# Transposing two slabs by whole 128x128 products instead of 32-row strips, with fewer filler products and another written order

## The chip, the core and the metric

The kernel runs on one core of a Trainium2 chip. The core has TensorE (matrix products into PSUM, written PE in the profile, its weight loads PEld), VectorE (DVE), ScalarE (ACT), GpSimd (POOL) and SyncE (SP), which here only issues DMAs. Each engine works through its own list of instructions in order and waits on semaphores for the others. The metric is the device time of one execution in microseconds (us).

## What is computed

Two layers, each an attention block and a gated block, over 2048 rows of 512 values in bfloat16; both layers use the same weights.

```python
x = x + A(layernorm(x));  x = x + B(layernorm(x))      # twice

# A: 32 heads of 16
q, k, v = split(x @ wqkv)
pq, pk  = q @ w_phi, k @ w_phi                         # per head
phi     = concat(softmax(p), softmax(-p))              # 32 features for q and for k
kv, z   = sum_s phi_k^T v, sum_s phi_k
o       = (phi_q @ kv) / (phi_q . z + 1e-6)
A       = o @ wo

# B
gate = x @ W_gate;  up = x @ W_up
B    = (relu(gate) * up) @ W_down
```

Attention is linear: the sums `kv` and `z` need all rows of keys and values before any row of the output can be made.

## The kernel before

The 2048 rows are 16 tiles of 128 rows, grouped into five slabs of 2, 4, 4, 4 and 2 tiles (`SLABS`). Slabs are numbered 0 to 4, layers 0 and 1. A stage is named by its layer and slab: `a01` is the normalization ahead of the attention of layer 0, slab 1; `g12` that ahead of the gated block of layer 1, slab 2.

At the start the kernel folds `w_phi` into the key and query weights (`fold`): it transposes the weights (keys by TensorE, queries by DMA), multiplies them by a block diagonal of `w_phi`, and evicts the results into `Wkp` and `Wqp`. Ahead of that TensorE runs eight warming products (`warm`, L788) and two groups of fillers (`filler`, L793, products of 256 columns whose result nobody reads): 8 before the fold and 10 after the fold of the keys.

`layernorm` (L862 to L908) takes a slab's tiles: statistics on VectorE (L847, L872), the reciprocal deviation on ScalarE (L874, L876), and the normalization of each tile into `ytile` on the engine that the table `ENG` names under `ap/...` (L889 or L892; on ScalarE it needs one small VectorE instruction more, L881). The normalized tile must then lie transposed in `yA` or `yG`. There are three ways: a DMA transpose from SyncE's queue (stages in `XPOSE`); for steps of several tiles `strips` (L910 to L930), which turns the tiles with 32x32 transposes at four row positions, 16 for each tile, into four banks, each bank then evicted by one copy that `ENG` places under `yc/...`; for steps of one tile, four 128x128 transposes into one bank (L713) and one copy. Before the change the strips are used by `a01` and `a02`: 64 transposes each (L921). All four copies of the strips together complete every tile; a tile's copy in the third way completes that tile alone.

`keys` makes, tile by tile, keys and values (L709 with `Wkp` and `wv`, eight products of 512 columns), exponentials on ScalarE (L949), their sums by a reduction on VectorE (L955), reciprocals (L958, or L961 and L962 on ScalarE by `rz/...`), the value eviction (`vc/...`), and the scaled values (L969, on GpSimd or VectorE by `vh/...`); then TensorE sums keys times values in 32 small products a tile (L981). For tile 9 of layer 0 the reduction is replaced by two DMA transposes and eight products on TensorE (`sums_by_pe`, L999 and L1007, by `zk/9`). `queries` (L1050) and `attend` follow, the gated block is `glu`.

The order of the instructions is settled while the kernel is built. `Program.schedule` (L446) plays the operations through with a cost for each; among those that can start it takes the one that starts first and, of equals, the one with the lowest number in `TURNS`, one number for each operation. The lists of the five engines come out in the order of the planned starts, and `plan` adds the semaphore waits. The planner has a cost for TensorE's instructions, which come in pieces: it takes a new piece to be there `FETCH0` ns after the piece before was entered, or `FETCH` ns once its clock is past 25 us. `LATE` is added to the planned landing of DMA transposes and some other DMAs. These numbers emit nothing; they only move the order.

Of the kernel before, what the change touches and what calls it, by code (L numbers as in the profile page):

```python
# [23 lines left out]
ENG = {'ap/a00/0': 'act',  # L24
 'ap/a01/1': 'dve',
# [4 lines left out]
 'ap/a03/3': 'dve',  # L30
 'ap/a10/0': 'act',
 'ap/a10/1': 'pool',
 'ap/a11/0': 'pool',
 'ap/a11/3': 'act',
 'ap/a12/1': 'pool',
 'ap/a12/3': 'act',
 'ap/a13/3': 'act',
 'ap/a14/1': 'act',
 'ap/g01/0': 'act',
 'ap/g01/1': 'act',  # L40
 'ap/g02/0': 'act',
 'ap/g02/1': 'act',
 'ap/g02/3': 'act',
 'ap/g03/0': 'act',
 'ap/g03/2': 'act',
# [3 lines left out]
 'ap/g12/3': 'act',  # L49
 'ap/g13/0': 'act',  # L50
 'ap/g14/1': 'act',
# [7 lines left out]
 'es/02/1': 'pool',  # L59
 'es/03/0': 'pool',  # L60
 'es/03/3': 'pool',
 'es/04/1': 'pool',
 'es/04/3': 'pool',
 'es/12/0': 'pool',
 'es/12/2': 'pool',
 'es/12/3': 'pool',
 'es/13/0': 'pool',
 'es/13/1': 'pool',
 'es/13/3': 'pool',
 'fck1': 'act',  # L70
 'fck2': 'dve',
 'fck3': 'act',
 'fcq2': 'dve',
 'ftk2': 'dve',
 'ftk3': 'act',
 'ld/wphi': 'sp',
 'ms/BD': 'pool',
 'ms/ZO 0': 'pool',
 'ms/kvs eps 0': 'pool',
 'ms/kvs eps 1': 'pool',  # L80
# [3 lines left out]
 'ot/00/3': 'act',  # L84
 'ot/01/0': 'dve',
 'ot/02/2': 'dve',
 'ot/03/0': 'dve',
 'ot/04/1': 'dve',
 'ot/04/2': 'dve',
 'ot/04/3': 'dve',  # L90
 'ot/11/0': 'dve',
 'ot/11/2': 'dve',
 'ot/12/2': 'dve',
 'ot/12/3': 'dve',
 'ot/13/0': 'dve',
 'ot/13/2': 'dve',
 'ot/13/3': 'dve',
 'ot/14/2': 'dve',
 'rz/0/1': 'act',
 'rz/0/12': 'act',  # L100
 'rz/0/13': 'act',
# [4 lines left out]
 'rz/0/6': 'act',  # L106
 'rz/0/7': 'act',
 'rz/1/14': 'act',
 'rz/1/15': 'act',
 'rz/1/2': 'act',  # L110
 'rz/1/4': 'act',
 'rz/1/6': 'act',
 'rz/1/7': 'act',
 'rz/1/8': 'act',
 'vc/0/11': 'dve',
 'vc/0/2': 'dve',
 'vc/0/5': 'dve',
 'vc/0/8': 'dve',
 'vc/1/12': 'dve',
 'vc/1/7': 'dve',  # L120
 'vc/1/8': 'dve',
 'vh/0/10/0': 'dve',
 'vh/0/11/0': 'dve',
 'vh/0/12/0': 'dve',
 'vh/0/13/0': 'dve',
# [5 lines left out]
 'vh/0/4/0': 'dve',  # L131
 'vh/0/5/0': 'dve',
 'vh/0/5/1': 'dve',
 'vh/0/7/1': 'dve',
 'vh/1/0/0': 'dve',
 'vh/1/11/0': 'dve',
 'vh/1/12/0': 'dve',
 'vh/1/12/1': 'dve',
 'vh/1/13/0': 'dve',
 'vh/1/14/0': 'dve',  # L140
 'vh/1/15/0': 'dve',
 'vh/1/15/1': 'dve',
 'vh/1/2/0': 'dve',
 'vh/1/2/1': 'dve',
 'vh/1/3/0': 'dve',
 'vh/1/4/0': 'dve',
 'vh/1/5/0': 'dve',
 'vh/1/5/1': 'dve',
 'vh/1/6/1': 'dve',
 'vh/1/8/0': 'dve',  # L150
# [5 lines left out]
 'yc/a01/03': 'act',  # L156
# [11 lines left out]
 'yc/a14/1': 'dve',  # L168
 'yc/g00/1': 'dve',
# [5 lines left out]
 'yc/g10/0': 'dve',  # L175
# [6 lines left out]
 'za/03': 'dve',  # L182
 'za/11': 'dve',
 'za/12': 'dve',
 'zk/9': 'pe'}
# [422 lines left out]
def build_kernel(nc, A_x, A_wqkv, A_w_phi, A_wo, W_gate, W_up, W_down, out):  # L608
# [8 lines left out]
    with ExitStack() as ctx:  # L617
# [86 lines left out]
        def bank(name):  # L704
            return Bank(name, pb)
# [13 lines left out]
        def b16half(ps):  # L719
            return ps.b16()[:, 0:512]  # L720
# [671 lines left out]
```

## Time and profile before

| | us |
|---|---|
| three runs | 388.72, 388.75, 387.99 |
| median | 388.72 |
| profiled execution | 388.32 |
| its span | 386.5 |
| TensorE busy | 371.2 |
| VectorE busy | 277.8 |
| ScalarE busy | 196.1 |
| GpSimd busy | 66.5 |

The span runs from the first to the last instruction of the profile; the profiled execution has its own time, 1.8 us above the span. In the lines of the profile that follow, a line of the timeline gives the start, the duration, the engine, the line of the kernel, what is written from what, a count, and in brackets the idle time of the engine before it with what ended that time. A line of the waits gives who waited for whom, the total, the number of times and the longest. A line of the windows gives the stretch, its length, and for TensorE's products, TensorE's weight loads, VectorE, ScalarE and GpSimd the busy time and in brackets the number of instructions; then the clock granted to TensorE, the busy share of the DMA engines, and GB/s.

### The profile page before, as it was taken

The page shows a single profiled execution, that of the slowest core. Times are in us where ns is not written, and L with a number is a line of the kernel's source. Part 1 is how long each engine was busy: PE and PEld are TensorE (multiplying, and loading weights), DVE is VectorE, ACT ScalarE, POOL GpSimd, SP SyncE. Part 2 cuts the span into 40 slices and gives each one's busy share as a digit, 9 for nine tenths or more (in the row PEclk, how much of TensorE's full clock was granted, in tenths as well). Part 3 has the DMA queues.
Part 4 walks back from the last instruction along what each step waited for, and adds up shares of the span by engine and source line. Part 5 has one row for each costly group of instructions (what it writes and reads, how often), then busy time and mean ns, then how long its engine had stood idle before and what let it go on. Part 6 is the DMA issues. An engine that isn't in the chain of part 4 may idle for free.

```text
span 386.5 us, 9068 instructions
## 1 busy us (share of the span) xinstructions
PE 371.2 (96%) x3743; PEld 197.6 (51%) x3793; DVE 277.8 (72%) x566; ACT 196.1 (51%) x433; POOL 66.5 (17%) x59
## 2 busy tenths in 40 slices
PE   7898999999999999999999999999999999999996
PEld 4453555484445444454457555466444444454574
DVE  7998998995856775974769797688865465743333
ACT  5998879752553434532535398982444113323111
POOL 2081730020502500120024031005024000000000
PEclk9999999999999999999999999999999999999999
DMA  7993402053661020202100310314562140230011
GB/s 227 303 323 67 70 5 55 25 156 61 139 97 52 22 54 3 54 15 54 27 4 2 62 29 6 83 42 136 102 151 70 44 83 1 44 91 16 2 41 50
DMA packets 58058, 27.72 MB, mean 72 GB/s; under 512 B 40384, under 2 KB 56352, under 8 KB 58016
## 3 DMA queue, kind: packets, MB, share of 16 engines
q1 hardware_dynamic: 57584, 26.77, 28.9%
q8 instruction: 30, 0.49, 0.6%
q10 hardware_dynamic: 432, 0.36, 0.3%
q14 instruction: 12, 0.10, 0.1%
HBM read 14.73 MB, written 4.00 MB: 48 GB/s over the span
## 4 chain that ended last, share of the span: by engine, by line
PE 86%; ACT 5%; DVE 3%; DMA 2%; issue 2%; SPq 1%; DVEq 0%; ACTq 0%
PE pb L709 82%; ACT expq L1050 2%; PE pb L981 2%; DMA hT<-in_A_wqkv_dram 1%; PE pb L1139 1%; DMA yG<-ytile 1%; DVE x_sb L1209 1%; ACT vsb L823 1%; ACT abT L823 1%; DVE stats L847 0%; PE pb L1078 0%; ACT expk L949 0%; ACT ytile L889 0%; SPq L732 0%; DVE hT L1263 0%
## 5 line engine op out<-in xcount | busy, mean ns | idle before, releaser
L709 PE MATMUL pb<-Wd,hT 128*128 128x512 bf16 (+3 forms) x353 | 93.1, 372 | 0.9 <-issue 0.6
L709 PE MATMUL pb<-yG,Wu 128*128 128x512 bf16 (+1 forms) x393 | 92.8, 336 | 0.8 <-DVE yG L820 0.3
L709 PE MATMUL pb<-yG,Wg 128*128 128x512 bf16 (+1 forms) x393 | 91.8, 336 | 0.4 <-issue 0.2
L1261 ACT ACTIVATE gate_sb<-pb 128x512 bf16<-128x512 f32 x80 | 46.6, 596 | 84.4 <-PE pb L709 51.8
L1263 DVE TENSOR_TENSOR hT<-gate_sb,pb 128x512 bf16<-128x512 bf16 x80 | 53.3, 682 | 39.4 <-PE pb L709 29.3
L1209 DVE TENSOR_TENSOR x_sb<-x_sb,pb 128x512 bf16<-128x512 bf16 x59 | 39.3, 680 | 23.2 <-PE pb L709 23.0
L709 PEld LDWEIGHTS pb<-yG,Wu 128*128 128x128 bf16 x400 | 39.0, 98 | 31.9 <-issue 0.5
L709 PEld LDWEIGHTS pb<-yG,Wg 128*128 128x128 bf16 x400 | 38.6, 98 | 29.9 <-issue 0.8
L709 PEld LDWEIGHTS pb<-Wd,hT 128*128 128x128 bf16 (+1 forms) x363 | 34.8, 98 | 36.6 <-issue 0.9
L969 POOL TENSOR_TENSOR vhat<-vsb,rZk 128x544 bf16<-128x544 bf16 x26 | 28.1, 1101 | 107.8 <-ACT vsb L823 58.6
L847 DVE BATCH_NORM_STATS2 stats<-x_sb 128x6 f32<-128x512 bf16 x60 | 39.8, 679 | 0.5 <-DMA x_sb<-in_A_x_dram 0.2
L709 PE MATMUL pb<-wv,yA 128*128 128x512 bf16 x124 | 37.3, 379 | 0.3 <-issue 0.2
L709 PE MATMUL pb<-Wkp,yA 128*128 128x512 bf16 x122 | 36.3, 379 | 1.1 <-ACT vsb L823 0.6
L1050 ACT ACTIVATE expq<-pb 128x512 bf16<-128x512 f32 x64 | 34.9, 631 | 3.6 <-PE pb L709 3.4
L709 PE MATMUL pb<-yA,Wqp 128*128 128x512 bf16 (+1 forms) x150 | 32.8, 334 | 2.9 <-issue 2.4
L709 PE MATMUL pb<-wo_sb,oT 128*128 128x512 bf16 x122 | 35.1, 379 | 0.6 <-ACT oT L823 0.5
L1172 POOL TENSOR_TENSOR expq<-expq,abT 128x1024 bf16<-128x1024 bf16 (+1 forms) x11 | 21.3, 1947 | 82.4 <-DVE nmr L881 30.5
L949 ACT ACTIVATE expk<-pb 128x512 bf16<-128x512 f32 x40 | 22.1, 612 | 10.8 <-PE pb L709 10.6
L955 DVE TENSOR_REDUCE Zk<-expk 128x64 f32<-128x1024 bf16 x19 | 22.7, 1201 | 5.8 <-ACT expk L949 5.7
L889 ACT ACTIVATE ytile<-x_sb,nmr,rstd 128x512 bf16<-128x512 bf16 x27 | 21.4, 815 | 5.8 <-DVE nmr L881 5.8
L709 PEld LDWEIGHTS pb<-yA,Wqp 128*128 128x128 bf16 x160 | 14.2, 98 | 14.2 <-issue 3.1
L709 PE MATMUL pb<-Wl,yG 128*128 128x192 bf16 x128 | 20.1, 246 | 0.4 <-DVE stats L847 0.2
(109 smaller groups left out, 372.7 us busy)
## 6 DMA issues: line engine op xcount, KB each, us to landing
abT<-spread SPq DMA_DIRECT2D x32, 128.0 KB
out_dram<-x_sb SPq DMA_DIRECT2D x15, 128.0 KB, 1.7
x_sb<-in_A_x_dram SPq DMA_DIRECT2D x3, 512.0 KB
Wu<-in_B_W_up_dram SPq DMA_DIRECT2D x1, 1280.0 KB
Wg<-in_B_W_gate_dram SPq DMA_DIRECT2D x1, 1280.0 KB
Wd<-in_B_W_down_dram SPq DMA_DIRECT2D x1, 1280.0 KB, 13.7
sums_scr<-abT SPq DMA_DIRECT2D x5, 256.0 KB, 2.3
Zs<-sums_scr SPq DMA_DIRECT2D x5, 256.0 KB, 2.7
```

What stands on the lines that cost most here:

```text
L709: op("pe", lambda e: e.matmul(view(ps), lhsT, rhs, start=start, stop=stop), reads=reads, writes=[ps], occ=max(25.0, 0.4167 * n + 2.6), lat ...
L823: op("act", lambda e: e.activation(dst(), src(), ACT.Copy), reads=[ps] + reads, writes=writes, occ=115 + 0.714 * n, lat=240 + 0.714 * n, n ...
L847: op("dve", lambda e: e.bn_stats(stats[:, t, :], src()), reads=[res], writes=[R("st", t)], occ=580, lat=680, name=f"bn{t}")
L889: op("act", (lambda t, yb: lambda e: e.activation(ytile[:, yb, :], x_sb[:, t, :], ACT.Identity, bias=nmr[:, t, :], scale=rstd[:, t, :]))(t ...
L949: op("act", (lambda i, s, pk: lambda e: e.activation(expk(i)[:, s, :], full(pk), ACT.Exp, scale=1.0 - 2.0 * s))(i, s, pk), reads=[pk], wri ...
L955: op("dve", (lambda i, zb: lambda e: e.tensor_reduce(Zk[:, zb, :], expk(i).rearrange("p s (h f) -> p (s h) f", f=16), AX.X, ALU.add))(i, z ...
L969: op(eng, (lambda i, s, vb, rz: lambda e: e.tensor_tensor(vhat(i)[:, s], vsb[:, vb, :, :], rZk[:, rz, s * 32:(s + 1) * 32].unsqueeze(2).to ...
L1050: op("act", (lambda c0, s, ps: lambda e: e.activation(eqv(st)[:, c0:c0 + per, s, :], ps.f32()[:, 0:per * n].rearrange("p (c n) -> p c n", ...
L1172: op(eng, lambda e: e.tensor_tensor(part, part, abT[:, c].rearrange("p (s n) -> p s n", s=2)[:, :, 0:n], ALU.mult), reads=Re + [R("abT", c ...
L1209: op("dve", lambda e: e.tensor_tensor(x_sb[:, t, :], x_sb[:, t, :], full(ps), ALU.add), reads=[R("x", t), ps], writes=[R("x", t)], occ=597 ...
L1261: op("act", (lambda gb, pg, k: lambda e: e.activation(gate_sb[:, gb, 0:k], pg.f32()[:, 0:k], ACT.Relu))(gb, pg, k), reads=[pg], writes=[R( ...
L1263: op("dve", (lambda gb, hb, pu, k: lambda e: e.tensor_tensor(hT[:, hb, 0:k], gate_sb[:, gb, 0:k], pu.f32()[:, 0:k], ALU.mult))(gb, hb, pu, k),
```

## The change

Two stages, `a01` and `a02`, are named in a new tuple `PLAIN`. `layernorm` no longer sends these through `strips`; it transposes each of their four tiles by four 128x128 products into a bank of its own and evicts that bank by one copy. The fillers after the fold of the keys go from 10 to 4, so that there are 12 and not 18. In the planner a piece of TensorE's instructions now counts as there 9000 ns after the piece before was entered if that was before 20 us of its clock, 6600 ns if before 29.5 us, and 3700 ns after. `LATE` goes from 300 to 400. `ENG` and `TURNS` are replaced: about a hundred operations move to another engine, and the order is written anew for all. `TURNS` itself is left out below.

```diff
 ENG = {
- 'ap/a00/0': 'act',
+ 'ap/a04/0': 'pool',
...
- 'ap/g01/0': 'act', 'ap/g01/1': 'act', 'ap/g02/0': 'act', 'ap/g02/1': 'act',
- 'ap/g02/3': 'act', 'ap/g03/0': 'act', 'ap/g03/2': 'act',
+ 'ap/g01/3': 'act', 'ap/g04/0': 'act', 'ap/g04/1': 'act',
...
- 'es/02/1': 'pool', 'es/03/0': 'pool', 'es/03/3': 'pool',
- 'es/12/0': 'pool', 'es/12/2': 'pool', 'es/13/0': 'pool',
+ 'es/13/2': 'pool', 'es/14/0': 'pool', 'es/14/1': 'pool', 'es/14/2': 'pool', 'es/14/3': 'pool',
- 'fck3': 'act', 'fcq2': 'dve', 'ftk2': 'dve',
+ 'ftk1': 'act', 'ld/x0': 'act',
- 'ms/ZO 0': 'pool', 'ms/kvs eps 0': 'pool', 'ms/kvs eps 1': 'pool',
+ 'ms/kvs 0 1': 'pool',
...
- 'vc/0/11': 'dve', 'vc/0/8': 'dve',
+ 'vc/0/3': 'dve', 'vc/0/4': 'dve', 'vc/0/9': 'dve',
...
- 'yc/a01/03': 'act',
+ 'yc/a01/03': 'dve',
+ 'yc/a02/00': 'dve', 'yc/a02/01': 'dve', 'yc/a02/02': 'dve', 'yc/a02/03': 'dve',
...
- 'zk/9': 'pe'}
...
+PLAIN = ()
...
-ZALL=(...); LASTCUT=((0,384),(384,512)); FILL=(8,10); LATE=300; LOADLATE=(150,200)
+ZALL=(...); LASTCUT=((0,384),(384,512)); LOADLATE=(150,200); FILL=(14,8); PLAIN=('a01','a02'); LATE=400; FILL=(8,4)
...
-    FETCH, FETCH0 = 3700.0, 9000.0
+    FETCH, FETCH1, FETCH0 = 3700.0, 6600.0, 9000.0
...
-                    came = crossed + (self.FETCH if at > 25000.0 else self.FETCH0) if chunk > self.CHUNK0 else 0.0
+                    came = crossed + (self.FETCH0 if crossed < 20000.0 else self.FETCH1 if crossed < 29500.0 else self.FETCH) if chunk > self.CHUNK0 else 0.0
...
-                elif step > 1:
+                elif step > 1 and key not in PLAIN:
                     strips(key, gi, b, r0, ybs)
                 else:
-                    ps = bank(f"ytr{t0}")
-                    for c in range(NC):
-                        tr(ps, ..., ytile[:, ybs[0], c * 128:(c + 1) * 128], [R("y", ybs[0])], f"ytr{t0}")
-                    evict(ENG.get(f"yc/{key}/{gi}", "act"), ..., 512, ps, [], R_yT(b, r0), f"ycp{t0}", False)
+                    for j, yb in enumerate(ybs):
+                        ps = bank(f"ytr{t0 + j}")
+                        for c in range(NC):
+                            tr(ps, ..., ytile[:, yb, c * 128:(c + 1) * 128], [R("y", yb)], f"ytr{t0 + j}")
+                        evict(ENG.get(f"yc/{key}/{gi}" + (f"{j}" if step > 1 else ""), "act"), ..., 512, ps, [], R_yT(b, r0 + j), f"ycp{t0 + j}", False)
                 t0 += step
```

Where `ENG` has no entry, a default holds: in the strips of `a01` and `a02` VectorE for the copies, in the plain way ScalarE; VectorE for the normalization of `a00` and ScalarE for that of the other layer 0 attention stages; SyncE for the load of the first tile; VectorE for the small fills, for the reduction of tile 9 and for the odd evictions of the fold of the keys, ScalarE for the fold's other evictions; VectorE for the scaling of the queries (`es/...`) and for the normalization ahead of the gated block.

More of the change, by code (lines that the diff above doesn't have):

```diff
@@ L23 @@
 HOLD = {}
-ENG = {'ap/a00/0': 'act',
- 'ap/a01/1': 'dve',
+ENG = {'ap/a01/1': 'dve',
  'ap/a01/2': 'dve',
@@ L33 @@
  'ap/a11/0': 'pool',
- 'ap/a11/3': 'act',
- 'ap/a12/1': 'pool',
+ 'ap/a11/1': 'pool',
+ 'ap/a12/0': 'act',
+ 'ap/a12/2': 'act',
  'ap/a12/3': 'act',
[L37 to L45, printed above, removed]
+ 'ap/a13/0': 'act',
+ 'ap/a13/2': 'pool',
+ 'ap/g01/3': 'act',
+ 'ap/g04/0': 'act',
+ 'ap/g04/1': 'act',
  'ap/g11/0': 'act',
@@ L48 @@
  'ap/g11/3': 'act',
- 'ap/g12/3': 'act',
- 'ap/g13/0': 'act',
- 'ap/g14/1': 'act',
+ 'ap/g12/0': 'act',
+ 'ap/g12/1': 'act',
+ 'ap/g13/2': 'act',
+ 'ap/g14/0': 'act',
  'em/01/01': 'dve',
@@ L58 @@
  'em/11/03': 'dve',
- 'es/02/1': 'pool',
- 'es/03/0': 'pool',
- 'es/03/3': 'pool',
+ 'em/11/13': 'dve',
  'es/04/1': 'pool',
  'es/04/3': 'pool',
- 'es/12/0': 'pool',
- 'es/12/2': 'pool',
  'es/12/3': 'pool',
- 'es/13/0': 'pool',
  'es/13/1': 'pool',
+ 'es/13/2': 'pool',
  'es/13/3': 'pool',
+ 'es/14/0': 'pool',
+ 'es/14/1': 'pool',
+ 'es/14/2': 'pool',
+ 'es/14/3': 'pool',
  'fck1': 'act',
  'fck2': 'dve',
- 'fck3': 'act',
- 'fcq2': 'dve',
- 'ftk2': 'dve',
+ 'ftk1': 'act',
  'ftk3': 'act',
  'ld/wphi': 'sp',
+ 'ld/x0': 'act',
  'ms/BD': 'pool',
- 'ms/ZO 0': 'pool',
- 'ms/kvs eps 0': 'pool',
- 'ms/kvs eps 1': 'pool',
+ 'ms/kvs 0 1': 'pool',
  'ot/00/0': 'dve',
@@ L83 @@
  'ot/00/2': 'dve',
[L84 to L87, printed above, removed]
+ 'ot/01/1': 'dve',
+ 'ot/01/2': 'dve',
+ 'ot/01/3': 'dve',
+ 'ot/02/1': 'dve',
+ 'ot/03/2': 'dve',
+ 'ot/03/3': 'dve',
  'ot/04/1': 'dve',
- 'ot/04/2': 'dve',
  'ot/04/3': 'dve',
- 'ot/11/0': 'dve',
+ 'ot/10/0': 'dve',
+ 'ot/10/3': 'act',
  'ot/11/2': 'dve',
- 'ot/12/2': 'dve',
- 'ot/12/3': 'dve',
- 'ot/13/0': 'dve',
+ 'ot/12/0': 'dve',
+ 'ot/13/1': 'dve',
  'ot/13/2': 'dve',
  'ot/13/3': 'dve',
- 'ot/14/2': 'dve',
+ 'ot/14/0': 'dve',
+ 'ot/14/3': 'dve',
  'rz/0/1': 'act',
+ 'rz/0/11': 'act',
  'rz/0/12': 'act',
- 'rz/0/13': 'act',
  'rz/0/14': 'act',
@@ L105 @@
  'rz/0/5': 'act',
- 'rz/0/6': 'act',
  'rz/0/7': 'act',
+ 'rz/0/9': 'act',
+ 'rz/1/0': 'act',
+ 'rz/1/10': 'act',
+ 'rz/1/11': 'act',
+ 'rz/1/12': 'act',
+ 'rz/1/13': 'act',
  'rz/1/14': 'act',
  'rz/1/15': 'act',
- 'rz/1/2': 'act',
+ 'rz/1/3': 'act',
  'rz/1/4': 'act',
[L112 to L115, printed above, removed]
+ 'rz/1/5': 'act',
  'vc/0/2': 'dve',
+ 'vc/0/3': 'dve',
+ 'vc/0/4': 'dve',
  'vc/0/5': 'dve',
- 'vc/0/8': 'dve',
- 'vc/1/12': 'dve',
- 'vc/1/7': 'dve',
+ 'vc/0/9': 'dve',
+ 'vc/1/0': 'dve',
+ 'vc/1/10': 'dve',
+ 'vc/1/11': 'dve',
+ 'vc/1/13': 'dve',
+ 'vc/1/15': 'dve',
+ 'vc/1/4': 'dve',
  'vc/1/8': 'dve',
  'vh/0/10/0': 'dve',
- 'vh/0/11/0': 'dve',
- 'vh/0/12/0': 'dve',
- 'vh/0/13/0': 'dve',
+ 'vh/0/10/1': 'dve',
+ 'vh/0/12/1': 'dve',
  'vh/0/13/1': 'dve',
@@ L130 @@
  'vh/0/15/1': 'dve',
- 'vh/0/4/0': 'dve',
- 'vh/0/5/0': 'dve',
- 'vh/0/5/1': 'dve',
+ 'vh/0/3/1': 'dve',
  'vh/0/7/1': 'dve',
- 'vh/1/0/0': 'dve',
- 'vh/1/11/0': 'dve',
+ 'vh/0/8/0': 'dve',
+ 'vh/0/8/1': 'dve',
+ 'vh/1/0/1': 'dve',
+ 'vh/1/1/1': 'dve',
+ 'vh/1/10/0': 'dve',
+ 'vh/1/11/1': 'dve',
  'vh/1/12/0': 'dve',
- 'vh/1/12/1': 'dve',
- 'vh/1/13/0': 'dve',
+ 'vh/1/13/1': 'dve',
  'vh/1/14/0': 'dve',
+ 'vh/1/14/1': 'dve',
  'vh/1/15/0': 'dve',
@@ L143 @@
  'vh/1/2/0': 'dve',
- 'vh/1/2/1': 'dve',
  'vh/1/3/0': 'dve',
  'vh/1/4/0': 'dve',
- 'vh/1/5/0': 'dve',
  'vh/1/5/1': 'dve',
- 'vh/1/6/1': 'dve',
- 'vh/1/8/0': 'dve',
+ 'vh/1/7/0': 'dve',
  'vh/1/9/0': 'dve',
@@ L155 @@
  'xp/g11': 'sp',
- 'yc/a01/03': 'act',
+ 'yc/a01/03': 'dve',
+ 'yc/a02/00': 'dve',
+ 'yc/a02/01': 'dve',
+ 'yc/a02/02': 'dve',
+ 'yc/a02/03': 'dve',
  'yc/a03/00': 'act',
@@ L168 @@
  'yc/a14/1': 'dve',
+ 'yc/g00/0': 'dve',
  'yc/g00/1': 'dve',
@@ L174 @@
  'yc/g04/02': 'dve',
- 'yc/g10/0': 'dve',
  'yc/g10/1': 'dve',
@@ L181 @@
  'za/02': 'dve',
- 'za/03': 'dve',
- 'za/11': 'dve',
  'za/12': 'dve',
- 'zk/9': 'pe'}
+ 'za/14': 'dve'}
 XPOSE = ()
@@ L324 @@
 FILL = (0, 0)
+PLAIN = ()
 XPOSE=("a02","a03","a04","a11","a12","a13","g01","g02","g03","g12","g13","g04","g14")
-ZALL=((0,2),(0,3),(0,4),(1,1),(1,2),(1,3),(1,4)); LASTCUT=((0,384),(384,512)); FILL=(8,10); LATE=300; LOADLATE=(150,200)
+ZALL=((0,2),(0,3),(0,4),(1,1),(1,2),(1,3),(1,4)); LASTCUT=((0,384),(384,512)); LOADLATE=(150,200); FILL=(14,8); PLAIN=('a01','a02'); LATE=400; FILL=(8,4)
 ENGINES = ("sp", "act", "pe", "dve", "pool")
@@ L898, in layernorm @@
                             reads=[R("y", yb)], writes=R_yT(b, r0 + j), nbytes=131072, name=f"ytx{t0 + j}", issue=XISSUE, delay=XDELAY + LATE)
-                elif step > 1:
+                elif step > 1 and key not in PLAIN:
                     strips(key, gi, b, r0, ybs)
                 else:
-                    ps = bank(f"ytr{t0}")
-                    for c in range(NC):
-                        tr(ps, (lambda c: lambda p: p.b16()[:, c * 128:(c + 1) * 128])(c), ytile[:, ybs[0], c * 128:(c + 1) * 128], [R("y", ybs[0])], f"ytr{t0}")
-                    evict(ENG.get(f"yc/{key}/{gi}", "act"), (lambda b, r0: lambda: yT(b)[:, :, r0 * 128:(r0 + 1) * 128])(b, r0),
-                          (lambda ps: lambda: b16half(ps).rearrange("p (c n) -> p c n", c=NC))(ps), 512, ps, [], R_yT(b, r0), f"ycp{t0}", False)
+                    for j, yb in enumerate(ybs):
+                        ps = bank(f"ytr{t0 + j}")
+                        for c in range(NC):
+                            tr(ps, (lambda c: lambda p: p.b16()[:, c * 128:(c + 1) * 128])(c), ytile[:, yb, c * 128:(c + 1) * 128], [R("y", yb)], f"ytr{t0 + j}")
+                        evict(ENG.get(f"yc/{key}/{gi}" + (f"{j}" if step > 1 else ""), "act"), (lambda b, r: lambda: yT(b)[:, :, r * 128:(r + 1) * 128])(b, r0 + j),
+                              (lambda ps: lambda: b16half(ps).rearrange("p (c n) -> p c n", c=NC))(ps), 512, ps, [], R_yT(b, r0 + j), f"ycp{t0 + j}", False)
                 t0 += step
```

245 rows, old and new, of the table TURNS are left out of this document.

## The prediction

> **What bounds the kernel now.** First the page's head and its engine line, then the chain of work that ended last.
>
> ```profile
> span 386.5 us, 9068 instructions
> PE 371.2 (96%) x3743; PEld 197.6 (51%) x3793; DVE 277.8 (72%) x566; ACT 196.1 (51%) x433; POOL 66.5 (17%) x59
> PE 86%; ACT 5%; DVE 3%; DMA 2%; issue 2%; SPq 1%; DVEq 0%; ACTq 0%
> ```
>
> TensorE is the bound: 96% busy, 86% of the chain. So the time falls only where TensorE stands idle or does work that can go. The list of who TensorE waits for says where it stands:
>
> ```profile
> PE pb L709 <- issue: 3.9, 16, 1.5
> PE pb L709 <- ACT vsb L823: 0.8, 2, 0.6
> PE pb L709 <- DVE Wqp L820: 0.4, 1, 0.4
> ```
>
> The longest wait in the middle of the work, 1.5 us, is put down to "issue": it waits for nothing that the profile shows. The chain in order of time and TensorE's timeline place it, and the two other waits above:
>
> ```profile
> 28.38 0.71 PE pb L709 x4
> 29.09 1.48 issue
> 30.57 8.15 PE pb L709 x38
> ...
> 2.03 3.13 PE L788 MATMUL pb<-yG 128*128 128x512 bf16 x7 [2.03 <-DVE yG L773]
> ...
> 12.25 1.03 PE L709 MATMUL pb<-Wkp,yA 128*128 128x512 bf16 x4
> 13.99 0.38 PE L793 MATMUL pb<-Wkp,yG 128*128 128x256 bf16 x2
> 14.30 0.66 PE L921 MATMUL pb<-ident,ytile 32*128 32x32 bf16 x64
> 15.37 0.62 PE L709 MATMUL pb<-hT 128*128 128x128 bf16 x8 [0.41 <-DVE Wqp L820]
> 16.59 1.03 PE L709 MATMUL pb<-Wkp,yA 128*128 128x512 bf16 x4 [0.60 <-ACT vsb L823]
> ...
> 27.57 0.65 PE L921 MATMUL pb<-ident,ytile 32*128 32x32 bf16 x64
> ```
>
> Both transpositions that change (L921, 64 products each) stand right ahead of idle time. What is the 1.48 us? The DMA answer for 27 to 29 us and the table of windows:
>
> ```profile
> q8 instruction: 1, 0.02, 4.1%
> ...
> 0.00:14.25 14.25, 11.74 (x85) 6.57 (x86) 12.12 (x41) 9.85 (x20) 2.27 (x11) 1.00 0.95 239
> 14.25:14.98 0.73, 0.70 (x66) 0.56 (x64) 0.73 (x2) 0.73 (x3) 0.00 (x0) 1.00 1.15 313
> 14.98:24.98 10.00, 9.01 (x50) 4.41 (x51) 10.00 (x20) 10.00 (x25) 4.28 (x4) 1.00 1.07 339
> 24.98:25.70 0.72, 0.70 (x65) 0.66 (x66) 0.72 (x4) 0.72 (x3) 0.30 (x1) 1.00 1.11 342
> 25.70:29.10 3.40, 3.05 (x80) 2.17 (x83) 3.40 (x7) 3.40 (x9) 3.40 (x4) 1.00 1.11 293
> ```
>
> Queue q8 moves "instruction" data: 30 packets, 0.49 MB in the run, 16 KB each; TensorE's 7,536 instructions over 30 make about 251 per piece. A piece moved just before TensorE went on, while the DMA share was above 1.0. TensorE's counts (first two "x" of each row) sum to 171, 130, 101, 131, 163: 696 when it stopped. So I read the wait as TensorE out of instructions: the piece asked for 251 earlier, at 445, is not there. 445 falls in slab 0's products of keys and values, 402 to 533, about 25.2 us; use began at 30.57, 5.4 us later. The wait stops the others too: ScalarE's timeline has 1.44 us idle before 30.98 us, for TensorE.
>
> **The change part by part.** The sum is made against the profiled execution, 388.32 us (span 386.5 and 1.8 around it); the median of the three runs, 388.72, is 0.4 above.
>
> *Instructions and the wait at 29 us.* A slab's 64 products of 32 columns become 16 of 128, and each comes with a weight load: 96 instructions fewer per slab, and 12 fewer for six fillers, 204 in all, 108 of them gone before 25 us. By 29.1 us TensorE then has issued 492. In the order of before, the windows 30.5 to 38.6 us and 38.6 to 40.1 us add 75 and 259, so 696 falls at about 39.4 us; 445 falls where before counted 553, near 27 us. The piece has 12 us where it took 5.4. Gain 1.5, bounds 1.5 and 0 (if the wait has another cause). What is late next is ScalarE's and VectorE's work; from 30 to 57 us they have 3.6 and 2.5 us idle, so they can follow.
>
> [...]
>
> *The wait at 15 us.* One strip transposition needs all four normalized tiles (the last from ScalarE at 14.02 us) and its evictions came at 15.23 to 16.31 us, behind an eviction of the folded weight. Tile by tile, the two that VectorE finished at 12.94 us can be turned and evicted at once. The two waits, 0.41 and 0.60, are the most there is; ScalarE and VectorE are busy 19.2 and 20.0 of the 20 us from 10 to 30, so not all comes. Gain 0.7, bounds 1.0 and 0.
>
> *TensorE's cost of the transpositions.* Four of 128 columns take 0.39 us with 0.22 the last one's own: 57 ns each, 16 in 0.91 us. A strip set lies 0.81 us ahead of the next product (27.57 to 28.38). Cost 0.1 a slab, 0.2; bounds 0 and 0.8 (the four-column evictions land no sooner).
>
> *Tile 9's sums.* They leave TensorE (8 products at L1007, 0.24 idle and 0.21 to the next product, 0.45) and two DMA transposes with 3.66 us of SyncE's queue; VectorE takes a reduction of 1.20 us. The cover is VectorE's 2.5 us idle from 30 to 57 us, 1.4 of it made by the wait above; without cover it costs up to 1.2. Gain 0.3, bounds 0.45 and minus 1.2.
>
> *Six fillers.* 0.11 us each, 0.65. They stand at 9.25 to 14.2 us, where TensorE otherwise waits for folded weights (ScalarE's until 10.64 us) and normalized tiles: 0, bounds 0.65 gained and 0 lost, unless the clock falls (below).
>
> *First load to ScalarE's queue.* SyncE's issues behind it come 0.43 us earlier, ScalarE's two weight columns as much later. 0, bounds 0.43 either way.
>
> *Other engine moves, to 57 us.* VectorE gets an eviction of a folded weight and one of the values (0.68 each), a normalization (0.41), tile 9 (1.20), small fills (0.2), 3.2 us; it gives up three evictions of the fold (0.42, 0.42, 0.68), two of slab 1's transposition (0.36 each), a scaled value (0.64), a fill (0.28) and two small scalars (0.18), 3.3 us. ScalarE gets five evictions (0.5 to 0.6 each, 2.7) and gives two evictions and two normalizations (2.7). GpSimd gets tile 14's normalization, 2.07 us where ScalarE took 0.81; its cover is the 8.39 us idle before 40.06 us. Later VectorE takes six scalings of queries from GpSimd, gives it five, and takes normalizations from ScalarE; it is busy 58 of the 80 us from 70 to 150, TensorE 79.5. All 0, bounds 0.5 either way.
>
> *The planner's fetch times and LATE* emit no instruction; they act by the order alone.
>
> Sum: minus 1.5, minus 0.7, plus 0.2, minus 0.3: minus 2.3. 388.32 minus 2.3 is 386.0; from the median 386.4. I put down 386.2.
>
> **The rivals.**
> *The wait stays or comes back elsewhere.* If it is no lack of instructions, or if the new order puts two sets of key-value products (128 instructions in 0.7 us) close behind each other and stops once more, 1.5 is not gained: 387.7. For: every slab has such sets; against: between 56 and 62 us 224 small products (448 instructions) ran with no wait over 0.2 us.
>
> *The gain is given back.* From 57 to 70 us ScalarE is busy 12.51 of 13.00 us and TensorE idle 1.7: ScalarE bounds that stretch. If it cannot start earlier, what was won ahead ends there: 388.5. Against: it has 3.6 us idle from 30 to 57.
>
> *Tile 14 on GpSimd, slower.* Its values' scalings take 1.10 us each and came four in a row from 46.23 us. If the normalization falls behind three of them, it is 1.26 plus 3.3 late, 4.6, and the keys of tile 14 wait: 390.6. It decides from 3.1 us late. Against: the idle 8.39 us.
>
> *TensorE's clock falls, slower.* The first seven products of 512 columns came 0.42 apart (3.13 us, the last lasting some 0.6), later ones 0.22 (1.03 us for four, the last 0.38): it begins at half pace. With fewer fillers, half pace from 9.2 to 16.6 us would cost 3.7: 389.7; it decides from 6.2 us at half pace. Against: the longest idle time from 5 to 29 us is 0.6. [...]
>
> **How the numbers follow.** Forecast 0.62 (its own range 385.0 to 387.3: the waits at 29 and 15 us gained between 1.2 and 2.5, the small terms either way). Wait stays 0.14, given back 0.12, GpSimd 0.08, clock 0.04. A measurement of this kernel tells some 0.2%, 0.8 us, from no change: faster is below 387.95, slower above 389.5. Faster 0.62 and 0.14, same 0.12, slower 0.12. The range 385.0 to 388.8 leaves out the slower cases and a little below.
>
> **What would show it.** Right: no "issue" wait over 0.5 us between 25 and 45 us; L921 gone, 16 products of 128 columns per slab in its place; idle before slab 1's first keys near 0.3 us; slab 2's and all later work 2 us earlier, and still so at the end. Wrong: an "issue" wait of 1 us or more at another place; TensorE idle over 3 us from 57 to 70; products 0.42 us apart after 9 us; a wait of keys for tile 14.

## The result and the profile after

| | before | after |
|---|---|---|
| median, us | 388.74 (387.99 to 389.02, 6 runs) | 386.69 (385.76 to 387.60, 6 runs) |
| profiled execution, us | 388.32 | 386.13 |
| its span, us | 386.5 | 384.4 |

The ratio is 0.9949, with a 95% interval of 0.9930 to 0.9969: faster by half a percent. From one profiled execution to the other it is 2.19 us, where the sum said 2.3; from median to median it is 2.05.

First the page of the kernel after: its head, the engines, the chain of work that ended last, and the queue that moves TensorE's instructions.

```profile
span 384.4 us, 8815 instructions
PE 372.3 (97%) x3630; PEld 200.1 (52%) x3683; DVE 278.2 (72%) x565; ACT 190.9 (50%) x431; POOL 66.8 (17%) x60
PE 77%; DVE 9%; ACT 6%; DMA 3%; issue 2%; POOL 1%; SPq 1%; ACTq 0%; DVEq 0%
q8 instruction: 29, 0.48, 0.5%
```

TensorE issues 223 instructions less (113 products, 110 weight loads) and still has 1.1 us more of busy time. Its idle time is what fell: span less busy time was 15.3 us and is 12.1. Minus 3.2 and plus 1.1 give the 2.1 by which the span is shorter. TensorE's waits say which idle time went (the line of the products, 709 before, is 716 here):

```profile
PE pb L716 <- issue: 1.6, 10, 0.2
PE pb L720 <- DMA hT<-in_A_wqkv_dram: 0.7, 1, 0.7
```

The longest wait put down to "issue" is 0.2 us where it was 1.5, and a wait of 0.7 us for a weight column is new. TensorE's timeline at the start, in the columns of the lines of before:

```profile
1.93 2.74 PE L795 MATMUL pb<-yG 128*128 128x512 bf16 x6 [1.93 <-DVE kvsum L788]
5.39 0.58 PE L720 MATMUL pb<-ident,hT 128*128 128x128 bf16 x4 [0.72 <-DMA hT<-in_A_wqkv_dram]
...
7.24 1.91 PE L800 MATMUL pb<-yG 128*128 128x256 bf16 x8
...
12.18 1.03 PE L716 MATMUL pb<-wv,yA 128*128 128x512 bf16 x4
...
15.55 0.33 PE L720 MATMUL pb<-ident,ytile 128*128 128x128 bf16 x3
...
28.67 0.68 PE L989 MATMUL pb<-vhat,expk 128*32 128x34 bf16 x64
```

Two things are to be seen. The strips are gone, and slab 1's whole products (three of them in the fifth row) lie between other products with no idle time in brackets. And the first products of keys and values start at 12.18 us, 1.94 later than before (10.24): TensorE waits 0.72 us for a weight column, whose load now stands behind the first tile's on ScalarE's queue, and the eight fillers of 256 columns take 1.91 us, at half the pace that products of that width have later (eight in 1.05 us at 65.33).

The windows, in the columns of the lines of before. Before:

```profile
0.00:10.00 10.00, 7.49 (x61) 4.62 (x63) 7.88 (x28) 5.99 (x12) 2.27 (x11) 1.00 0.79 233
10.00:30.00 20.00, 17.71 (x286) 9.74 (x287) 20.00 (x46) 19.15 (x44) 8.56 (x8) 1.00 1.12 304
30.00:60.00 30.00, 28.39 (x623) 15.15 (x628) 26.89 (x49) 25.99 (x64) 11.82 (x11) 1.00 0.22 41
60.00:70.00 10.00, 8.48 (x206) 4.33 (x206) 9.26 (x24) 9.94 (x24) 0.00 (x0) 1.00 0.21 56
```

After:

```profile
0.00:10.00 10.00, 7.34 (x34) 3.96 (x35) 7.92 (x29) 4.09 (x9) 2.14 (x9) 1.00 0.82 255
10.00:30.00 20.00, 19.70 (x208) 12.41 (x210) 19.12 (x46) 19.97 (x47) 6.49 (x6) 1.00 1.13 301
30.00:60.00 30.00, 28.71 (x683) 14.90 (x688) 28.32 (x50) 27.86 (x70) 17.05 (x15) 1.00 0.13 26
60.00:70.00 10.00, 9.49 (x180) 4.66 (x174) 9.84 (x22) 9.07 (x20) 0.00 (x0) 1.00 0.18 54
```

TensorE's idle time falls from 2.29 to 0.30 us between 10 and 30 us, from 1.61 to 1.29 between 30 and 60, and from 1.52 to 0.51 between 60 and 70. The same milestones in both traces say how much of this counts: the 20th product of keys and values begins 0.1 us earlier (17.51, then 17.40), the first product with `ZA`, at the start of the attention's output, 2.03 earlier (61.72, then 59.69), the first with `wo_sb` 2.83 earlier (69.71, then 66.88), and TensorE's last 2.14 earlier (382.92, then 380.78). So next to nothing is won before 17 us, some 2 us between 17 and 60, and after 70 us 0.7 of what was won goes again. The granted clock of 1.00 in the first row of each table says nothing of the very start: the traces have no clock record ahead of 4.98 us before and of 11.18 us after, and the column shows 1.00 there.

### The profile page after: what moved, and what is told of

Same layout as the page of the kernel before. It is cut to its first block, busy times and chain, and to the rows that moved or that the text cites. A ratio compares the mean times of both kernels' runs of the same rounds, so it can differ in the third digit from the quotient of the medians.

```text
span 384.4 us, 8815 instructions
## 1 busy us (share of the span) xinstructions
PE 372.3 (97%) x3630; PEld 200.1 (52%) x3683; DVE 278.2 (72%) x565; ACT 190.9 (50%) x431; POOL 66.8 (17%) x60
## 4 chain that ended last, share of the span: by engine, by line
PE 77%; DVE 9%; ACT 6%; DMA 3%; issue 2%; POOL 1%; SPq 1%; ACTq 0%; DVEq 0%
PE pb L716 72%; DVE Zk L963 2%; PE pb L989 2%; DVE expq L1213 1%; PE pb L1147 1%; DMA abT<-spread 1%; ACT expk L957 1%; DMA hT<-in_A_wqkv_dram 1%; DVE stats L854 1%; ACT expq L1058 1%; SPq L1135 1%; DVE oT L827 1%; ACT ytile L896 1%; ACT yA L830 1%; DVE ytile L899 1%
## 5 line engine op out<-in xcount | busy, mean ns | idle before, releaser
L716 PE MATMUL pb<-yG,Wg 128*128 128x512 bf16 (+1 forms) x396 | 97.0, 336 | 0.5 <-issue 0.2
L716 PE MATMUL pb<-yG,Wu 128*128 128x512 bf16 (+1 forms) x391 | 96.1, 335 | 0.7 <-issue 0.2
L716 PE MATMUL pb<-Wd,hT 128*128 128x512 bf16 (+4 forms) x351 | 94.9, 372 | 0.8 <-issue 0.3
L1271 DVE TENSOR_TENSOR hT<-gate_sb,pb 128x512 bf16<-128x512 bf16 x80 | 54.1, 683 | 46.9 <-PE pb L716 30.1
L977 POOL TENSOR_TENSOR vhat<-vsb,rZk 128x544 bf16<-128x544 bf16 x25 | 27.3, 1104 | 91.8 <-DVE rZk L966 30.6
L1058 ACT ACTIVATE expq<-pb 128x512 bf16<-128x512 f32 x64 | 35.5, 626 | 1.6 <-PE pb L716 1.4
L1180 POOL TENSOR_TENSOR expq<-expq,abT 128x512 bf16<-128x512 bf16 (+1 forms) x10 | 15.3, 1544 | 96.9 <-DMA abT<-spread 37.5
L963 DVE TENSOR_REDUCE Zk<-expk 128x64 f32<-128x1024 bf16 x20 | 23.9, 1205 | 1.8 <-ACT expk L957 1.8
L1237 ACT ACTIVATE gate_sb<-pb 128x192 bf16<-128x192 f32 x16 | 5.3, 328 | 32.3 <-PE pb L716 32.3
L716 PEld LDWEIGHTS pb<-yA,Wqp 128*128 128x128 bf16 x160 | 14.4, 98 | 12.1 <-issue 1.4
L896 ACT ACTIVATE ytile<-x_sb,nmr,rstd 128x512 bf16<-128x512 bf16 x22 | 17.6, 829 | 3.9 <-DVE nmr L888 3.8
```

The source lines that it names most:

```text
L716: op("pe", lambda e: e.matmul(view(ps), lhsT, rhs, start=start, stop=stop), reads=reads, writes=[ps], occ=max(25.0, 0.4167 * n + 2.6), lat ...
L896: op("act", (lambda t, yb: lambda e: e.activation(ytile[:, yb, :], x_sb[:, t, :], ACT.Identity, bias=nmr[:, t, :], scale=rstd[:, t, :]))(t ...
L963: op("dve", (lambda i, zb: lambda e: e.tensor_reduce(Zk[:, zb, :], expk(i).rearrange("p s (h f) -> p (s h) f", f=16), AX.X, ALU.add))(i, z ...
L977: op(eng, (lambda i, s, vb, rz: lambda e: e.tensor_tensor(vhat(i)[:, s], vsb[:, vb, :, :], rZk[:, rz, s * 32:(s + 1) * 32].unsqueeze(2).to ...
L1058: op("act", (lambda c0, s, ps: lambda e: e.activation(eqv(st)[:, c0:c0 + per, s, :], ps.f32()[:, 0:per * n].rearrange("p (c n) -> p c n", ...
L1180: op(eng, lambda e: e.tensor_tensor(part, part, abT[:, c].rearrange("p (s n) -> p s n", s=2)[:, :, 0:n], ALU.mult), reads=Re + [R("abT", c ...
```

## The experiments

The written order answers to every edit, since the planner chooses anew. So in all the kernels here the choice is replaced by a fixed sequence, that of the kernel edited, with the sequence written into `TURNS`; every engine keeps its old order except at the edit.

```diff
-            wide = [(o.prio, o.ready) for o in ready["pe"] if len(new_banks(o)) > 1]
...
-            _, _, o, s = best
+            o = min((o for e in ENGINES for o in ready[e]), key=lambda o: o.prio)
```

Runs that are compared with one another share the runs of the kernel before. Medians of those were 388.89 us (29 runs) for the first four kernels, 389.09 (14) for the next four and 389.14 (35) for the last four.

**The transposition alone, in the order of before (`b_plain`, `b_plain2`).** Slabs 1 and 2, or slab 2 only, by whole products where the strips stood; the copies stay on their engines; all 18 fillers, all other engines and the order are those of before.

```diff
+PLAIN = ('a01', 'a02')          # b_plain2: ('a02',)
...
-                elif step > 1:
+                elif step > 1 and key not in PLAIN:
```

> The kernel before, its order of instructions kept, with slab 1 and slab 2 transposed by whole products in the strips' place (192 of TensorE's instructions fewer). Theory (TensorE runs out of instructions at 29 us): the 1.48 us wait at 29 us is gone and the transpositions cost 0.1 a slab more, 1.3 us faster, 387.4. Rival (the wait has another cause; the gain came from the new order): the wait stays, 388.9.

> The same for slab 2 alone (96 instructions fewer); slab 1 keeps its strips. Theory: what counts is that slab 2's 128 instructions and those of slab 0's key-value products fall into one piece; the wait is gone with the one slab too, 387.4. Rival (what counts is the sum of instructions before 25 us): most of the wait stays, 388.5 or more.

Measured: 388.19 us for both slabs (387.48 to 389.51, 12 runs; ratio 0.9983, 0.9966 to 0.9999) and 388.10 for slab 2 alone (387.32 to 389.23, 12 runs; 0.9983, 0.9969 to 0.9997). The wait at 29 us is gone from both traces, and the time falls by 0.7 us, less than half of it. TensorE's timeline of the kernel with both slabs shows where the rest went:

```profile
41.01 0.59 PE L677 MATMUL pb<-Wkp,yA 128*128 128x512 bf16 x2 [0.92 <-DMA yA<-ytile]
...
58.37 0.30 PE L950 MATMUL pb<-oT,abT 128*32 128x34 bf16 x20 [0.70 <-issue]
```

The 48th product of keys and values is 1.7 us earlier than before (31.9, then 30.2), the 96th 0.6 (44.4, then 43.8), the first with `ZA` 0.2 (61.72, then 61.55). 0.92 us goes to slab 3, whose rows a DMA transposes and which are not there yet, 0.70 to a new wait of the old kind among small products. In the kernel with slab 2 alone the second of these is larger. Its timeline and its windows there:

```profile
50.91 0.53 PE L946 MATMUL pb<-vhat,expk 128*32 128x34 bf16 x45
52.57 0.30 PE L946 MATMUL pb<-vhat,expk 128*32 128x34 bf16 x19 [1.13 <-issue]
```

```profile
49.90:51.44 1.54, 1.54 (x143) 1.26 (x141) 1.54 (x3) 1.13 (x5) 0.78 (x1) 1.00 0.00 0
51.44:52.57 1.13, 0.00 (x1) 0.00 (x0) 1.13 (x3) 0.55 (x3) 0.32 (x1) 1.00 0.00 0
```

And the windows of the kernel with both slabs, up to its wait and in it:

```profile
55.30:57.67 2.37, 2.21 (x142) 1.56 (x143) 2.37 (x5) 1.35 (x4) 0.00 (x0) 1.00 0.02 7
57.67:58.37 0.70, 0.00 (x1) 0.00 (x1) 0.02 (x1) 0.70 (x3) 0.00 (x0) 1.00 0.00 0
```

In the kernel with slab 2 alone TensorE issued 284 instructions (143 products and 141 weight loads) in 1.54 us, stood 1.13 us in the middle of a row of 64 equal products, and went on. The DMA share was 0.00. So the wait needs no load on the DMA queues.

Two readings say that it is one for instructions. In the kernels' own lists (a product and its weight load count two, each further wait of an operation one) TensorE stops within three instructions of 702 in the kernel before, of 1,470 in `b_plain2` and of 1,726 in `b_plain`: 3 and 4 times 256 further on. And the traces' DMA records have one 16 KB instruction packet ahead of the end of each wait: it lands at 29.25, 51.22 and 56.94 us, and TensorE goes on 1.3 to 1.4 us later each time (30.57, 52.57, 58.37). Taking out 96 instructions moved other work onto the edges of the pieces, which removes the wait in one place and can make one in another.

**A burst of small products, near and far (`a_burst_near`, `a_burst_far`).** The order after, with 120 small products (240 instructions) whose result nobody reads: once right behind slab 0's products of keys and values, while weights load, once in the gated block of layer 0.

```diff
+                def idle_products(e):
+                    for j in range(30):
+                        for i in range(4):
+                            ins = e.matmul(burst.f32()[32 * i:32 * i + 32, 0:34], ident[:, 32 * i:32 * i + 32], ident[:, 0:34], start=True, stop=True, ...)
+                    return ins
+                op("pe", idle_products, reads=[R("ident")], writes=[burst], occ=1100, lat=1228, name="burst", mode=1, ins=120)
```

> The changed kernel with 120 small idle products (240 instructions, of the shape of the key-value products, on the identity) right after slab 0's key-value products, so that nearly a whole piece is used up within 2 us. They leave nothing that is read. Theory: their own 1.1 us, and a wait of TensorE for the next piece of 2.5 to 4 us: 390 to 392. Rival (no lack of instructions): their own time alone, 387.8.

> The same 120 idle products in the gated block of layer 0, at about 118 us, some ten us after a piece was entered and as long before the next end of a piece. Theory: no wait for instructions, only their own time of 1.1 us and two changes of the shape of products at some 0.2 each: 388.2. Rival: the same as with the products at 30 us.

Measured: near 392.95 us (391.95 to 393.98, 4 runs; ratio 1.0104, 1.0080 to 1.0129), far 388.52 (387.02 to 391.24, 10 runs; 0.9999, 0.9974 to 1.0024). The chain of the near one in order of time, and two of its windows:

```profile
28.71 0.61 PE pb L947 x64
29.32 1.08 PE pb L962 x112
30.41 3.66 issue
34.06 0.25 PE pb L962 x8
```

```profile
24.00:29.20 5.20, 5.15 (x104) 3.65 (x102) 5.20 (x11) 5.18 (x12) 3.91 (x4) 1.00 1.08 341
33.00:39.80 6.80, 5.52 (x23) 2.39 (x24) 4.28 (x10) 2.65 (x6) 2.16 (x2) 0.50 0.10 22
```

The wait could be made at will, and in the size worked out for it (2.5 to 4 us); the whole time came out above the 390 to 392 us expected. TensorE stopped after 112 of the 120 products, at 702 instructions again. Counted 256 instructions back from there (224 of the burst, and 32 that belong to the last 16 of the 64 products ahead), the piece was entered at about 29.0 us, and the next was used at 34.06: 5.1 us, with a DMA share of 1.08 before. In `b_plain2` the same count gives entry at about 50.1 and use at 52.57, 2.5 us, and in `b_plain` 55.3 and 58.37, 3.1 us, both with next to no other transfers. These are estimates from the rows. So the time from entering one piece to having the next was about twice as long while the weights load (5.1 here, 5.4 in the kernel before). The DMA records say where it went: the packet began 1.6 us behind the entry here and 2.8 in the kernel before, within 0.8 us of it in the other two, and it took 2.2 us here and 0.9 to 1.4 in the other three. That the loads are the reason is argued from these four stops; no run took the loads away. The second window shows the rest of the price: the granted clock was 0.50 for 6.8 us, from 33.0 us on, 2.6 us after TensorE had stopped (30.41).

The far burst made TensorE wait no more than 0.16 us, as its timeline says:

```profile
122.37 1.39 PE L962 MATMUL pb<-ident 128*32 128x34 bf16 x120
123.92 0.81 PE L674 MATMUL pb<-Wd,hT 128*128 128x512 bf16 x3 [0.16 <-issue]
```

Counted on in steps of 256 from the near burst's stop at 702 instructions, in which the stops at 1,470 and 1,726 lie too, the far burst begins at about 2,887 and has the edge at 3,006 in its middle, with products of 512 columns on either side. So this pair shows that as many instructions cost 3.66 us in one place and almost nothing in another; it does not separate the load from the place in the piece. For the load there are the four stops above. The profiled execution of the far kernel is the slowest of its ten (391.24 us); its first product with `ZA` comes at 62.01 us, 2.3 later than in the kernel after, so a good part of what it lost was lost ahead of the burst.

**The start (`a_x0`, `a_warm10`).** The order after, with the loads of the start as before (the first tile's on SyncE's queue, the last slab's behind the weights), or with two more warming products ahead of the first weight column.

```diff
- 'ld/x0': 'act',               # a_x0
...
-        NWARM = 8
+        NWARM = 10              # a_warm10
```

> The changed kernel with the loads of the start on the queues and in the sequence they had before (the first tile's load on SyncE's queue, ScalarE's queue begins with the two weight columns). In the changed kernel's profile TensorE waits 0.72 us for a weight column and works at half pace until 11.2 us, where before it was 5.0 us. Theory (the load ahead of the weight column made TensorE idle and its clock late): TensorE doesn't wait, works at full pace from 5 to 6.5 us, slab 0's first keys or values come at 10.5 us where the changed kernel has 12.2, and the time is 0.5 to 1.5 us below the changed kernel, ratio to the kernel before 0.991 to 0.9935. Rival (the clock's start is chance, or the start is covered by ScalarE and VectorE behind it): the changed kernel's ratio, 0.995.

> The changed kernel with two warming products more, ten, the two placed into TensorE's idle time ahead of the first weight column. Theory (idle time holds the clock down): full pace from 5 to 6.5 us, 0.5 to 1.2 us below the changed kernel. Rival (the weight column's delay itself costs): no change from the changed kernel's ratio of 0.995, or 0.3 us more.

Measured: 387.61 us (387.15 to 388.46, 8 runs; ratio 0.9963, 0.9949 to 0.9977) and 387.72 (386.49 to 387.79, 7 runs; 0.9952, 0.9933 to 0.9971). Both do at the start what they should. A row of each timeline, the first products of keys and values (12.18 us in the kernel after), `a_x0` and then `a_warm10`:

```profile
10.99 1.03 PE L673 MATMUL pb<-wv,yA 128*128 128x512 bf16 x4 [0.40 <-DMA wv<-in_A_wqkv_dram]
```

```profile
11.18 1.03 PE L674 MATMUL pb<-wv,yA 128*128 128x512 bf16 x4
```

And neither ends earlier: the first product with `ZA` comes at 60.47 and 60.03 us, where the kernel after had it at 59.69. The theory that the late start costs time at the end is not borne out. `a_warm10` is not a clean test of it. Its two products more move every later edge, and at 57.73 us, again within three instructions of the 1,726th, TensorE stands 0.95 us; the profile puts this down to ScalarE, but ScalarE then waits 0.96 us for TensorE, and an instruction packet landed 1.4 us before the end of the wait, as in the stops above.

**The kernel after once more (`a_again`), and tile 14 on ScalarE (`a_ap14`).** The first is unchanged but for the fixed sequence. The second undoes one engine move:

```diff
- 'ap/a04/0': 'pool',
```

> The changed kernel itself, beside the next two on one chip. Its instructions on every engine are those of the changed kernel in the same order. Its ratio to the kernel before should be 0.993 to 0.997 again; its profile shows whether the late full pace of TensorE (11.2 us) is a property of the kernel or changes from run to run, with the time of the first attention sums (59.7 us) unmoved if ScalarE and VectorE bound the start.

> The changed kernel with tile 14 of layer 0 normalized on ScalarE (0.81 us) as before and not on GpSimd (2.07 us), in the place that it has in the order. Theory (GpSimd's part is covered, and ScalarE, busy 9.5 of 10 us from 30 to 40 us, pays 0.8): 0 to 0.8 us above the changed kernel. Rival (tile 14 comes late from GpSimd): 0.5 us or more below it.

Measured: 387.77 us (386.31 to 389.28, 12 runs; ratio 0.9959, 0.9936 to 0.9982) and 387.51 (385.86 to 389.76, 12 runs; 0.9959, 0.9936 to 0.9982). Where tile 14 is normalized makes no difference that shows. The unchanged kernel says why an earlier start doesn't count: in this execution TensorE was at full pace from 4.8 us without any edit, and its first keys came at 11.09. Its timeline there, later on, and two windows:

```profile
7.22 1.04 PE L758 MATMUL pb<-yG 128*128 128x256 bf16 x8
...
34.52 0.59 PE L674 MATMUL pb<-Wkp,yA 128*128 128x512 bf16 x2 [1.26 <-DMA yA<-ytile]
```

```profile
30.00:31.00 1.00, 1.00 (x7) 0.45 (x5) 1.00 (x4) 1.00 (x3) 1.00 (x2) 1.00 0.99 120
32.00:33.00 1.00, 1.00 (x6) 0.39 (x4) 1.00 (x2) 1.00 (x6) 0.47 (x1) 1.00 1.86 125
```

The 48th product of keys and values was 0.8 us earlier than in the first execution of this kernel (24.9, where that had 25.7), the 64th 0.7, and then TensorE stood 1.26 us for slab 3's DMA transposition, and the 80th was 0.7 later (36.2, where that had 35.5). The first execution has a DMA share of 0.31 between 30 and 31 us and 0.56 between 32 and 33, this one 0.99 and 1.86: the transfers lasted about 1 us longer, and the transposition landed late. `a_x0` stands at the same place, 0.74 us before 34.53, there for ScalarE. So in `a_again` and `a_x0` the earlier start is given back at 33 to 35 us.

**Fillers (`a_fill0`, `a_fill8`, `a_x0_fill0`).** The order after without any filler, without the late four only, and without any and with the loads as before.

```diff
-FILL=(8,4)
+FILL=(0,0)                      # a_fill8: (8,0)
```

> The changed kernel with no fillers (eight less at 7 to 9 us, four less at 70 to 75 us, where the written order put them). Theory (fillers stand on TensorE's way to the first keys, 0.21 us each at half pace): first keys or values 1 to 1.7 us earlier, time up to 1 us below the changed kernel. Rival (they bring the clock up): half pace lasts beyond 11.2 us, no gain or up to 2 us slower.

> The changed kernel without its four late fillers (70 to 75 us), the eight early ones kept. Theory (only the late ones lie on TensorE's path, four by 0.11 us): 0.4 us below the changed kernel, as much as with no fillers at all. Rival (the early ones cost as well): no fillers at all is another 0.3 us or more below this.

> Both edits, the loads as before and no fillers. Theory: with the clock up by 6.5 us the fillers cost only 0.11 us each, so 0 to 0.8 us below the loads' edit alone. Rival: without fillers the clock falls back or comes late, slower than the loads' edit alone by 1 us or more.

Measured: without any 386.06 us (385.18 to 386.97, 6 runs; ratio 0.9921, 0.9903 to 0.9939), without the late four 387.10 (386.30 to 388.74, 12 runs; 0.9950, 0.9928 to 0.9972), without any and with the old loads 386.91 (386.61 to 387.58, 6 runs; 0.9943, 0.9927 to 0.9958). Two rows of the timeline without fillers:

```profile
8.14 0.40 PE L678 MATMUL pb<-ident,hT 128*128 128x128 bf16 x4 [1.92 <-DMA hT<-in_A_wqkv_dram]
...
9.73 2.06 PE L674 MATMUL pb<-hT 128*128 128x128 bf16 x16 [0.26 <-POOL hT L776]
```

TensorE waits 1.92 us where the fillers stood and falls to half pace from 9.5 to 12.9 us (the 16 products in the second row take 2.06 us, 1.48 in the kernel after for the same ones at 10.65), and yet the first product with `ZA` comes at 59.63 us, 0.06 earlier than in the kernel after. Fillers buy nothing here. Nor does the half pace come from their absence. `a_fill8` keeps the eight early ones:

```profile
7.82 0.40 PE L678 MATMUL pb<-ident,hT 128*128 128x128 bf16 x4 [2.04 <-DMA hT<-in_A_wqkv_dram]
8.06 1.86 PE L758 MATMUL pb<-yG 128*128 128x256 bf16 x8
```

It waits 2.04 us for the same weight column, and its granted clock is 0.50 from 8.1 to 11.5 us; `a_burst_far`, with the same start, waits 2.24 and has 0.50 from 8.4 to 11.8. `a_again` waits 1.33 us there, `a_x0_fill0` 1.50 at its longest, and neither falls back. So in these five executions the fall goes with the length of that wait, 1.92 us and more against 1.50 and less, which differs from execution to execution.

Without any filler is the lowest median of all, but its interval overlaps that of the kernel after, so that it is better is not shown; nor do these runs tell early fillers from late ones. With the old loads, leaving them out gives 0.7 us less than `a_x0`, inside what its theory said, with intervals that overlap.

**Tile 9's sums on VectorE in the order of before (`b_zk9`).**

```diff
- 'zk/9': 'pe'}
+ }
```

> The kernel before with tile 9's sums made by VectorE (1.20 us) right after its exponentials, not by two DMA transposes and eight products. Theory (0.45 us of TensorE go, VectorE has cover): 0.3 us below the kernel before. Rival (VectorE is full in that stretch): up to 1.2 us above it.

Measured: 389.34 us (388.30 to 391.58, 12 runs; ratio 1.0012, 0.9991 to 1.0034): no gain, if anything a loss. The wait at 29 us is still there, 1.17 us long, and a new one stands later, larger than the 0.45 us of products that TensorE gives up. Two rows of its timeline:

```profile
30.44 0.81 PE L667 MATMUL pb<-yA,Wqp 128*128 128x256 bf16 x4 [1.17 <-issue]
...
47.41 0.66 PE L939 MATMUL pb<-oT,abT 128*32 128x34 bf16 x64 [1.17 <-POOL oT L927]
```

## Why the prediction was right, step by step

*The wait at 29 us, 1.5.* Right in cause and size. It is gone in the kernel after, in `b_plain` and in `b_plain2`, stays in `b_zk9`, and is made larger by the near burst. The step put the 445th instruction near 27 us and the 696th near 39.4; in the trace after, by its own order, they come at about 29.0 and 38.8, 9.8 us apart where the piece takes some 5 (5.1 and 5.4 in the estimates above). It is one crossing from piece to piece among many: the kernel before has 30 pieces, and no other wait put down to "issue" is above 0.25 us there. The crossings at which TensorE stopped cost 1.48 us there, 0.70 and 1.13 in the first two experiments, 3.66 with the burst.

*"They can follow."* Wrong as an argument, though not in the sum. The step took the 1.5 us for won at the end because ScalarE and VectorE had idle time from 30 to 57 us. In the order of before they have it too, and `b_plain` kept only 0.3 us in its profiled execution (388.32, then 387.99) and 0.7 in the medians (388.89, then 388.19). The rivals "the wait comes back elsewhere" and "the gain is given back" are what happens there, both at once: 0.70 us of new waiting for instructions, 0.92 for slab 3's transposition. The rest of the gain comes with the written order. The prediction gave the planner's new counts no price of their own, since they emit nothing; they move the order, and the order after has no wait for instructions above 0.2 us although its pieces have other edges. Which part of the new order does it was not isolated.

*The wait at 15 us, 0.7.* TensorE's 1.0 us of idle time there went, as said, but the step looked at it alone. The first keys came 1.94 us later, and the 20th product of keys and values is 0.1 earlier instead of 0.7. `a_x0`, `a_warm10` and `a_again` brought that start forward by some 1.0 to 1.2 us and got nothing at the end for it. The term is 0.1 measured, not 0.7.

*What made up for it.* Between 60 and 70 us TensorE's idle time fell by 1.0 us, for which the sum had no term: queries, quotients and scaled values come in another order there. It is in the milestones as 0.8 us (2.03 ahead at the first `ZA`, 2.83 at the first `wo_sb`), of which 0.7 goes again after 70 us. So the sum of 2.3 was nearly met by 2.19, with one term too large and the order's effect, which was put at nothing, in its place. That they agree to 0.1 us is luck: a term that was 0.6 too large was made up by stretches for which the sum had none, and the same kernel run again (`a_again`) gained 1.3 us from one profiled execution to the other (388.32, then 387.02) and 1.4 from median to median (389.14, then 387.77).

*Transposition, 0.2 on TensorE.* Not seen apart. 32 whole products in place of 128 small ones lie between other work, and the idle time that had stood around them is gone, the 0.3 us foreseen ahead of slab 1's keys too.

*Tile 9's sums, 0.3.* Not borne out. In the order of before the edit gains nothing; the new wait of 1.17 us is one for GpSimd, and the step had looked at VectorE's cover alone. In the new order it was not tried alone.

*Six fillers, first load, other moves, all 0.* The four late fillers that stay came at 70 to 75 us in the new order. Nothing speaks against these terms within what the runs can tell, 0.2 to 0.3%. For GpSimd's tile 14 the row that was missing is there: `a_ap14` and `a_again` have the same ratio, so that rival has no price here. For the first load, two executions that were both at full pace early (from 7.4 and 4.8 us) compare: the first keys come at 10.99 us without it (`a_x0`) and at 11.09 with it (`a_again`), inside the bounds of 0.43, and the ratios are 0.9963 and 0.9959.

*The clock.* This rival happened in part. The kernel after ran at half pace until about 11 us, so the sign that was named for it, half pace after 9 us, is there; the rival put that stretch from 9.2 to 16.6 and its turning point at 6.2 us. ScalarE and VectorE are busy 19.97 and 19.12 of the 20 us from 10 to 30, and the executions whose keys began 1 us earlier ended no sooner, so what TensorE lost to the half pace was not lost at the end. That goes only so far: where the keys began at 12.95 and 13.54 us (`a_fill8`, `a_burst_far`), the first product with `ZA` came at 60.60 and 62.01. What the prediction set against this rival, that the longest idle time was 0.6 us, was too weak: it was that of one execution of the kernel before, and waits of 1.92, 2.04 and 2.24 us at the start went with half pace in three executions. The new whole transposes brought no half pace: from 12 us on no more than four of them follow one another in the timeline of the kernel after, and the granted clock is 1.00 from 11.18 us to the last product.

## What to carry to other kernels

A wait put down to "issue" with no change of shape and no semaphore behind it may be a wait for instructions; here such waits were 0.70 to 3.66 us long, and those with a change of shape mostly 0.16. Count TensorE's instructions up to it: the stops here lay within three of 702, 1,470 and 1,726, multiples of 256 apart. Then count 256 back from it: from there to the end of the wait it was 2.5 and 3.1 us in this kernel, and 5.1 and 5.4 with a DMA share of 1.08 and more (estimates from the rows). See also whether an instruction packet landed just before it ended, 1.3 to 1.4 us here. Fewer and wider products ahead of it (16 of 128 columns for 64 of 32) took the 1.48 us away here. Removing it moves the edges of all later pieces, so look for its return (0.70 and 1.13 us here), and for the next DMA that the earlier work now meets (0.92 us). An earlier start of the bounding engine, by 1.0 to 1.2 us, was worth nothing here where the other engines were full behind it.

## What the runs showed of the hardware

The wait for instructions came with a DMA share of 0.00 too: 284 instructions in 1.54 us, then 1.13 us of nothing. I had taken the loads of weights for a condition; with them the time from entering a piece to having the next was about twice as long (5.1 and 5.4 us, against 2.5 and 3.1, estimates from the rows), and no more. From the landing of the instruction packet to TensorE's going on it was 1.3 to 1.4 us in all four.

The start of TensorE's full pace is not fixed by the instructions. The same list came to it at 4.8 us in one execution and at about 11 in another (eight products of 256 columns in 1.04 and in 1.91 us at the same place), where the first weight column landed 0.55 us later (5.39, against 4.84). It can be lost again early: in `a_fill8`, `a_burst_far` and `a_fill0` TensorE had it by 4.7 to 6.1 us, waited 2.04, 2.24 and 1.92 us, and was at half pace for 3.4 us from 8.1, 8.4 and 9.5 us on.
